# Visit 9 instead of visit 8 for the second rows' reciprocal, product and turns, in an attention and feed-forward kernel on one Trainium2 core

## The chip, the cores and the metric

The kernel runs on one core of one Trainium2 chip. A core has TensorE (PE in the profile; PEld is its weight load), VectorE (DVE), ScalarE (ACT), GpSimd (POOL) and SyncE (SP), which here only issues DMAs. Results of PE land in a memory of eight banks, PSUM; DVE and ACT empty the banks. The metric is the device time of one execution in microseconds, as the median of several runs.

## The reference

Two attention steps on `x` (4 batches of 12480 tokens with 128 channels, 32 inducing rows), then a feed-forward layer with a leaky ReLU of 2048 units:

```python
def mab(q, kv):
    s = scale * (q @ kv.transpose(0, 2, 1))
    s = s - s.max(-1, keepdims=True)
    a = np.exp(s)
    a /= a.sum(-1, keepdims=True) + 1e-09
    return a @ kv
h = mab(I, x)               # I: the inducing rows, for each batch
y = mab(x, h)               # 4 x 12480 x 128
...
h = y @ w_in                # 49920 x 2048
g = np.maximum(h, 0.0) + alpha * np.minimum(h, 0.0)
return g @ w_out
```

## The kernel before, in words

**Rows, blocks, visits.** The tokens of a batch are cut into groups of 16 tiles of 128 tokens; the code calls one such group `(b, s)`: batch `b`, rows `s`. "First rows" is `(0, 0)`, "second rows" `(0, 1)`. A group has four blocks of four tiles (512 tokens). Each block is visited four times; a visit computes four chunks of 128 of the 2048 hidden units for the block's 512 tokens. Visits are numbered through: 0 to 15 are the first rows, 16 to 31 the second rows, and so on. The part ahead of visit 0 (loads, the first attention step of batch 0) is a list of steps written out by hand.

**One visit.** `visit` takes four banks (`hh`) and issues four matmuls side by side, each with 32 rows of the attention weights `a2` and of the product `HW` (inducing output times `w_in`), L808. Then the four banks are emptied with a ReLU into bf16 tiles `gt`, on ACT (L821) or DVE (L823). In the same turn of the loop `second` multiplies the `gt` of the visit before by the output weights, 16 matmuls (L834), into the block's accumulator bank `bp`. `linear` adds the linear part of the leaky ReLU for a pair of blocks (L861): at visit 8 for blocks 0 and 1, at visit 12 for blocks 2 and 3. So PE's order is: the four L808 of visit n, now and then L861, the sixteen L834 of visit n-1, then what the tasks of visit n add.

**Finishing a block.** `finish` reads the accumulator bank into an output tile `ob` and issues its DMA from SP (L894). For the first four blocks the attention weights are not yet normalised, so there `ob` is the accumulator times the reciprocal `rec` of the sums (DVE, L880); later blocks are plain copies. `rec` is made at visit 7 (DVE, L1173) from a tree of sums on POOL. `blocks[0].later` holds block 0 back: it is finished at visit 8, just before block 1, which `second` finishes in the same turn of the loop.

**Preparing the next rows.** While a group is visited, the attention weights of the next are made by eight tasks, each put at a visit: `b_scores` (16 small matmuls, L644, and a copy to SBUF), `b_max` (DVE, L721), `b_less_pool` (POOL, L726), `b_exp` (ACT, L688), `b_sum` (five additions on POOL, L712, and L736, which gives `den`), `b_rec` (the reciprocal `rc` of `den`, DVE, L749), `b_mul` (POOL, L758, makes `rep`, the weights repeated four times in bf16) and `b_turn` (a transposing DMA from SP, L766, into `a2`, whose tile is `a<-rep` in the profile). For the second rows product and turn come in two halves of eight tiles. The list `when` in the planning loop says at which visit each of the eight stands. Visit 16 is the first to read the second rows' `a2`, and only its first half; visit 24 is the first to read the other half.

**What decides the order.** Each engine runs its instructions in the order in which the program issues them; nothing is reordered at run time. A planner (`Plan.choose`) runs at build time: with a beam search over estimated costs it decides for each visit which of the four ReLUs go to ACT and which to DVE, on which engine a copy runs, whether a task's DVE or ACT work stands at the end of its visit ("n") or in the middle of the next visit's ReLUs ("l", run by `run_waiting` ahead of the third ReLU), and which of the eight banks each tile takes. Moving a task therefore may also change those choices nearby. A task's own semaphore waits are placed by the framework: an instruction that waits holds up what is behind it on its engine, and SP's DMAs are issued strictly one after the other.

Of the kernel before, what the change touches and what calls it, by code (L numbers as in the profile page):

```python
# [30 lines left out]
def kernel(  # L31
# [654 lines left out]
    def b_exp(e, n):  # L686
        def work():
            nc.scalar.activation(out=e[:, :n], in_=e[:, :n], func=EXP, scale=scale)  # L688

        plan.then(work)  # L690
# [512 lines left out]
    def at(n, fn, *args, cost=()):  # L1203


        todo.setdefault(max(n, 0), []).append((fn, args, cost))
# [12 lines left out]
    for b, s, nt in groups[1:]:  # L1219
        n = first[b, s]  # L1220
        when = [n - 23, n - 19, n - 16, n - 14, n - 13, n - 11, n - 9, n - 6]
        if (b, s) == (0, 1):
            when = [0, 2, 3, 6, 7, 8, 8, 8]
        if (b, s) == (0, 2):
            when[7] = n - 7
        at(when[0], on, b, b_scores, s, nt, cost=[("s", 25 * nt), ("f", 0)])
        at(when[1], on, b, b_max, s, nt, cost=[("v", 70 + 33 * nt)])
        at(when[2], on, b, b_less_pool, s, nt)
        at(
            when[3],  # L1230
            lambda b=b, s=s, nt=nt: b_exp(states[b].e2[s], nt),
            cost=[("a", 100 + 27 * nt)],
        )
        at(when[4], on, b, b_sum, s, nt)
        at(when[5], on, b, b_rec, s, nt, cost=[("v", 160)])
        parts = [(0, H), (H, H)] if (b, s) in ((0, 1), (0, 2)) else [(0, nt)]
        for t0, n in parts:
            at(when[6], on, b, b_mul, s, n, t0)
            if when[6] == when[7]:
                at(when[7], on, b, b_turn, s, t0, n)  # L1240
        if when[6] != when[7]:
            for t0, n in parts:
                at(when[7], on, b, b_turn, s, t0, n)
# [130 lines left out]
```

## Time and profile before

| | |
|---|---|
| median of 3 runs | 593.95 us (593.32, 593.95, 594.05) |
| the profiled execution's own time | 593.45 us |
| its span in the trace | 591.7 us |
| around the span | 1.75 us |
| granted TensorE clock | 0.999 of full speed |
| PE busy | 584.9 us (99%) |
| DVE, ACT busy | 534.6 us (90%), 537.8 us (91%) |
| POOL busy | 216.9 us (37%) |
| visit 0 starts at | 30.04 us of the span |

In the trace, times are counted from the start of the span. A row of the timeline has the start, the duration, the engine, the source line, the operation, the tiles written and read with their shapes, and how many equal instructions were merged into the row; in square brackets stands how long the engine was idle before it and who ended that. A q after an engine's name stands for its queue, where DMAs are issued. The chain of waits is followed back from the last instruction of the program: at each step to what released it, or to the instruction before it on its engine. A busy PE is not PE at its peak, since the ends of matmuls are modelled; the starts of successive rows tell the pace.

### The profile page before, as it was taken

The numbers are of one execution on the slowest core, as the hardware profiler recorded it, in microseconds if no ns is written. First come the engines' busy times: TensorE is split into PE (matmuls) and PEld (weight loads), VectorE is DVE, ScalarE is ACT, GpSimd is POOL, SyncE is SP. The second block draws the span as 40 slices with busy tenths as digits, with TensorE's granted clock in tenths as the row PEclk, the third lists the DMA queues.
The fourth block names the chain that finished last, engine by engine and source line by source line (L and its number), as shares of the span: only waits on it lengthen the run. The fifth ranks groups of instructions, "written<-read, shape, count | busy, mean of one in ns | idle before, by whom it ended". The sixth has DMA issues, their size and how long they took to land.

```text
span 591.7 us, 23147 instructions
## 1 busy us (share of the span) xinstructions
PE 584.9 (99%) x9500; PEld 441.2 (75%) x9500; DVE 534.6 (90%) x977; ACT 537.8 (91%) x1086; POOL 216.9 (37%) x262
## 2 busy tenths in 40 slices
PE   8999999999999999999999999999999999999997
PEld 6677777777777777777777777777777777777776
DVE  5889999998999899999999899999999899999996
ACT  5788999999999999998999999999998998999985
POOL 3484543523325426413226256124034134144110
PEclk9999999999999999999999999999999999999999
DMA  8957699533188999532257999741331331432421
GB/s 335 278 184 171 149 244 202 134 89 88 38 236 159 212 194 219 118 82 67 80 151 186 183 238 224 139 100 38 91 77 51 92 77 52 119 83 58 91 69 47
DMA packets 122411, 80.56 MB, mean 136 GB/s; under 512 B 103824, under 2 KB 106176, under 8 KB 119232
## 3 DMA queue, kind: packets, MB, share of 16 engines
q1 hardware_dynamic: 122080, 78.99, 55.0%
q8 instruction: 74, 1.21, 0.9%
q14 instruction: 33, 0.27, 0.2%
q10 hardware_dynamic: 224, 0.09, 0.1%
HBM read 28.07 MB, written 25.56 MB: 91 GB/s over the span
## 4 chain that ended last, share of the span: by engine, by line
PE 91%; DVE 1%; DVEq 0%; issue 0%; ACT 0%
PE bp L834 64%; PE hh L808 21%; PE bp L861 2%; PE hh L644 1%; PE hh L473 1%; PE hh L379 1%; DVE gt L823 0%; DVE ob L880 0%; DVEq L1369 0%; PE hh L598 0%; PE hh L521 0%; DVE s L393 0%; PE hh L582 0%; PE hh L567 0%; PE hh L518 0%
## 5 line engine op out<-in xcount | busy, mean ns | idle before, releaser
L821 ACT ACTIVATE gt<-hh 128x512 bf16<-128x512 f32 x852 | 454.4, 605 | 35.2 <-PE hh L808 29.6
L823 DVE TENSOR_SCALAR gt<-hh 128x512 bf16<-128x512 f32 x708 | 454.3, 684 | 25.1 <-PE hh L808 14.3
L834 PE MATMUL bp<-W,gt 128*128 128x128 bf16 x6240 | 417.1, 220 | 0.2 <-DVE gt L823 0.2
L834 PEld LDWEIGHTS <-gt 128*128 128x128 bf16 x6240 | 349.3, 98 | 84.9 <-issue 77.0
L808 PE MATMUL hh<-a,HW 32*128 32x512 bf16 (+2 forms) x1664 | 156.4, 370 | 0.3 <-DVE ob L880 0.2
L758 POOL TENSOR_TENSOR rep<-e,rc 128x2048 bf16<-128x2048 f32 (+2 forms) x26 | 84.8, 3263 | 24.6 <-DVE rc L749 24.2
L726 POOL TENSOR_TENSOR e<-e,smx 128x512 f32<-128x512 f32 (+1 forms) x24 | 24.6, 1025 | 155.8 <-ACT gt L821 73.2
L808 PEld LDWEIGHTS <-HW 32*128 32x128 bf16 x1664 | 40.4, 91 | 42.0 <-issue 6.2
L712 POOL TENSOR_TENSOR t<-e 128x256 f32<-128x256 f32 (+1 forms) x24 | 17.2, 717 | 140.1 <-ACT e L688 140.1
L887 ACT COPY ob<-bp 128x512 f32<-128x512 f32 x64 | 37.5, 585 | 4.6 <-PE bp L834 1.4
L712 POOL TENSOR_TENSOR t<-t 128x128 f32<-128x128 f32 (+3 forms) x100 | 30.3, 303 | 7.8
L330 POOL CAST xn<-xs 128x2048 bf16<-128x2048 f32 x17 | 32.1, 1888 | 2.1 <-DMA xs<-in_x_dram 1.6
L889 DVE COPY ob<-bp 128x512 f32<-128x512 f32 x30 | 20.6, 686 | 5.2 <-PE bp L834 5.2
L393 DVE TENSOR_SCALAR_CACHE_REDUCE s<-hh 128x512 f32<-128x512 f32 (+2 forms) x29 | 18.0, 619 | 1.6 <-PE hh L379 1.6
L861 PEld LDWEIGHTS <-a 32*128 32x128 bf16 x392 | 15.0, 93 | 5.7
L861 PE MATMUL bp<-HA,a 32*128 32x128 bf16 x392 | 19.1, 214 | 0.0
L418 ACT ACTIVATE e1T<-s,rm 128x512 bf16<-128x512 f32 (+1 forms) x25 | 18.0, 719 | 0.7 <-DVE rm L402 0.7
L721 DVE TENSOR_REDUCE smx<-e 128x16 f32<-128x512 f32 (+1 forms) x24 | 15.9, 662 | 0.0
L963 PE MATMUL bp<-blank 128*128 128x256 bf16 x78 | 14.2, 318 | 1.2 <-DVE blank L909 1.2
L688 ACT ACTIVATE e<-e 128x512 f32<-128x512 f32 (+1 forms) x24 | 15.0, 626 | 0.0
L489 DVE SCALAR_TENSOR_TENSOR hs<-hs,fac,hh 128x128 f32<-128x128 f32 (+1 forms) x25 | 8.6, 344 | 6.4 <-PE hh L473 5.8
L702 ACT COPY e<-hh 128x512 f32<-128x512 f32 (+1 forms) x22 | 13.4, 607 | 0.0
(109 smaller groups left out, 204.5 us busy)
## 6 DMA issues: line engine op xcount, KB each, us to landing
out_dram<-ob SPq DMA_DIRECT2D x97, 256.0 KB, 2.5
xs<-in_x_dram SPq DMA_DIRECT2D x23, 1024.0 KB, 6.4
xs<-in_x_dram SPq DMA_DIRECT2D x2, 512.0 KB, 9.0
w_in_f<-in_moe_w_in_dram SPq DMA_DIRECT2D x1, 1024.0 KB, 4.8
a<-rep SPq DMA_TRANSPOSE x27, 4.8
xT<-xn SPq DMA_TRANSPOSE x18, 6.4
e<-e1T SPq DMA_TRANSPOSE x18, 3.8
xs_left<-in_x_dram SPq DMA_DIRECT2D x4, 64.0 KB, 5.2
```

Source lines behind the costliest of these rows:

```text
L330: nc.gpsimd.tensor_copy(out=st.xn[s][:], in_=xs[:])
L393: nc.vector.tensor_scalar(out=s1[:parts, :cols], in0=ps[:parts, :cols], scalar1=-scale, scalar2=None, op0=MULT, op1=MIN, accum_out=st.mx[: ...
L712: nc.gpsimd.tensor_tensor(out=t[:, :n], in0=src[:, :n, :w], in1=src[:, :n, w : 2 * w], op=ADD)
L726: nc.gpsimd.tensor_tensor(out=st.e2[s][:, :n], in0=st.e2[s][:, :n], in1=st.m2[s][:, :n].unsqueeze(2).broadcast_to([P, n, M]), op=SUB,)
L758: nc.gpsimd.tensor_tensor(out=st.rep[s][:, ts], in0=st.e2[s][:, ts].unsqueeze(2).broadcast_to([P, n, R, M]), in1=rc[:, ts].unsqueeze(2).un ...
L808: nc.tensor.matmul(hh[:, q * cols + w.start : q * cols + w.stop], HWs[b][rows, v * P : (v + 1) * P], a2[rows, t0 : t0 + nt, :].rearrange(" ...
L821: nc.scalar.activation(out=gt[:, :cols], in_=hh[:, :cols], func=RELU)
L823: nc.vector.tensor_relu(gt[:, :cols], hh[:, :cols])
L834: nc.tensor.matmul(blk.acc[:, t * C : (t + 1) * C], gt[:, (q * nt + t) * P : (q * nt + t + 1) * P], W1[:, k, :], start=(not blk.begun), st ...
L861: nc.tensor.matmul(blk.acc[w, t * C : (t + 1) * C], blk.a2[rows, blk.t0 + t, w], HAs[b][rows, :], start=(not blk.begun and t == 0), stop=F ...
L887: nc.scalar.copy(out=ob[:, :nt], in_=acc)
L889: nc.vector.tensor_copy(out=ob[:, :nt], in_=acc)
```

## The change

The last three tasks of the second rows, `b_rec`, `b_mul` and `b_turn`, are put at visit 9 and not at visit 8. Their order among themselves stays, the halves are kept, and nothing else in the source differs.

```diff
         if (b, s) == (0, 1):
-            when = [0, 2, 3, 6, 7, 8, 8, 8]
+            when = [0, 2, 3, 6, 7, 9, 9, 9]
```

With that the built program has its instructions in another order near visits 7 to 10. The number of instructions is the same on every engine. Each row below is one engine's order, from the ReLUs of visit 7 to those of visit 10; the number in brackets is the visit of a ReLU.

```
DVE before: relu(7) relu(7) rec relu(8) relu(8) rc ob0 ob1 relu(9) relu(10) relu(10)
DVE after:  relu(7) relu(7) rec relu(8) ob0 ob1 relu(9) rc relu(10) relu(10)
ACT before: relu(7) exp relu(7) relu(8) relu(8) relu(9) x3 copy(scores) relu(10) x2
ACT after:  relu(7) relu(7) exp relu(8) x3 relu(9) x3 copy(scores) relu(10) x2
SP before:  turn xT, turn a first half, turn a second half, out block 0, out block 1, turn xT left, turn xT
SP after:   turn xT, out block 0, out block 1, turn a first half, turn a second half, turn xT left, turn xT
```

Here `exp` is the second rows' `b_exp`, `rc` their reciprocal, `ob0` and `ob1` the scaled outputs of blocks 0 and 1. The planner now puts `ob0` and `ob1` at the end of visit 8's own ReLUs, where before they stood in the middle of visit 9's. It also gives the first two ReLUs of visit 7 to ACT (before: the second and third) and the first three of visit 8 (before: the first two). Visit 9 and all visits from 10 on keep their division between ACT and DVE. The four `hh` banks of visit 10 were before, in order: one emptied by DVE in visit 8, that of block 0's accumulator, one emptied by ACT in visit 9, and that of block 1's accumulator. After the change they are one emptied by ACT in visit 8, one emptied by ACT in visit 9 (its first ReLU), that of block 1's accumulator, and another emptied by ACT in visit 9 (its second ReLU). From visit 12 on, all but eight tiles of some 1700 follow the same tile in their bank as before. POOL's order does not change at all.

## The prediction

> **What bounds the kernel now.** The page comes first: which engine fills the span, and what the chain of waits is made of.
>
> ```profile
> span 591.7 us, 23147 instructions
> PE 584.9 (99%) x9500; PEld 441.2 (75%) x9500; DVE 534.6 (90%) x977; ACT 537.8 (91%) x1086; POOL 216.9 (37%) x262
> PE 91%; DVE 1%; DVEq 0%; issue 0%; ACT 0%
> ```
>
> PE is the bound: 91% of the chain is its own. A change on DVE, POOL or SP is worth only what it takes from PE's waiting. So the second view is PE's own waits over the whole span (who was waited for; total, times, longest, in us).
>
> ```profile
> PE bp L963 <- DVE blank L909: 1.2, 1, 1.2
> PE hh L364 <- POOL w_in_f L1036: 0.7, 1, 0.7
> PE hh L808 <- DVE ob L880: 0.2, 1, 0.2
> PE bp L834 <- DVE gt L823: 0.2, 1, 0.2
> PE hh L967 <- ACT ind_b L956: 0.2, 1, 0.2
> ```
>
> L963, L967 and L364 belong to the hand-written part ahead of visit 0. In the visits there are two waits: one for a `gt` (L834) and one of L808 on `ob` (L880), which the diff touches. Its 0.2 us counts only the time without any running matmul, so I measure the hole by the pace of the visits, in the timeline around it.
>
> ```profile
> 41.92 0.39 PE L861 MATMUL bp<-HA,a 32*128 32x128 bf16 x8
> 42.23 1.07 PE L834 MATMUL bp<-W,gt 128*128 128x128 bf16 x16
> 43.23 0.40 PE L808 MATMUL hh<-a,HW 32*128 32x512 bf16 x4
> 43.56 1.07 PE L834 MATMUL bp<-W,gt 128*128 128x128 bf16 x16
> 44.95 0.86 PE L808 MATMUL hh<-a,HW 32*128 32x512 bf16 x3
> 46.02 0.37 PE L808 MATMUL hh<-a,HW 32*128 32x512 bf16 x1 [0.21 <-DVE ob L880]
> 46.32 1.07 PE L834 MATMUL bp<-W,gt 128*128 128x128 bf16 x16
> 47.32 0.40 PE L808 MATMUL hh<-a,HW 32*128 32x512 bf16 x4
> 48.65 0.40 PE L808 MATMUL hh<-a,HW 32*128 32x512 bf16 x4
> 54.17 0.40 PE L808 MATMUL hh<-a,HW 32*128 32x512 bf16 x4
> ```
>
> Visit 8 ends with the L834 at 42.23; visits 9, 10, 11, 12 start at 43.23, 44.95, 47.32, 48.65, and visit 16 at 54.17. Visit 11 takes 48.65 - 47.32 = 1.33 us, an undisturbed visit without extra work. Visit 10 has no extra work either, and takes 47.32 - 44.95 = 2.37 us. **The hole is 2.37 - 1.33 = 1.04 us.** Its four L808, issued together elsewhere (0.40 for all four), come out in pieces, the last at 46.02, because their banks come free late. What holds them is on the other engines:
>
> ```profile
> 42.03 0.24 DVE L1173 RECIPROCAL rec<-den 128x16 f32<-128x16 f32 x1
> 42.18 1.28 DVE L823 TENSOR_SCALAR gt<-hh 128x512 bf16<-128x512 f32 x2
> 44.57 0.25 DVE L749 RECIPROCAL rc<-den 128x16 f32<-128x16 f32 x1 [1.10 <-POOL den L736]
> 44.74 1.22 DVE L880 TENSOR_TENSOR ob<-bp,rec 128x512 f32<-128x512 f32 x2
> 45.88 3.99 DVE L823 TENSOR_SCALAR gt<-hh 128x512 bf16<-128x512 f32 x6
> 40.78 0.60 ACT L821 ACTIVATE gt<-hh 128x512 bf16<-128x512 f32 x1
> 41.28 0.62 ACT L688 ACTIVATE e<-e 128x512 f32<-128x512 f32 x1
> 41.80 1.56 ACT L821 ACTIVATE gt<-hh 128x512 bf16<-128x512 f32 x3
> 43.72 1.57 ACT L821 ACTIVATE gt<-hh 128x512 bf16<-128x512 f32 x3 [0.35 <-PE hh L808]
> 41.98 0.73 POOL L712 TENSOR_TENSOR t<-e 128x256 f32<-128x256 f32 x1 [1.06 <-ACT e L688]
> 42.78 1.46 POOL L712 TENSOR_TENSOR t<-t 128x128 f32<-128x128 f32 x4
> 44.96 3.75 POOL L758 TENSOR_TENSOR rep<-e,rc 128x1024 bf16<-128x1024 f32 x2 [0.43 <-issue]
> ```
>
> Read it backwards. L808 waits for `ob`, whose two products are done at 44.74 + 1.22 = 45.96. They could have run much earlier: `rec` is there at 42.27, block 0's accumulator is complete with the L861 at 42.31, block 1's with the L834 at 43.30. But on DVE they stand behind `rc`, and `rc` waits 1.10 us, until 44.57, for POOL's `den`, the end of a tree that started at 41.98, when ACT's `exp` had ended (41.28 + 0.62).
>
> **The change part by part.** No instruction is added or removed, so the sum has only moved waits. I follow the new order with the durations above, and a start-to-start step of 0.48 for ACT's ReLUs ((1.56 - 0.60)/2) and 0.60 for DVE's (1.28 less a ReLU's 0.68).
>
> *DVE.* After `rec` comes one ReLU of visit 8 (42.18), then `ob0` at 42.8, done 43.4, and `ob1`, which needs 43.30 and starts about 43.4, done 44.1. Then visit 9's ReLU, done 44.7. Both accumulator banks are free 1.9 us earlier than 45.96. The wait on `den` has not gone: it now stands in front of visit 10's ReLUs.
>
> *ACT and POOL.* Two ReLUs of visit 7 now precede `exp`, so `exp` is one step late: 41.76, and with it the tree, `den`, `rc` (45.05 to 45.30), the product (45.44) and the turns, all +0.48. Visit 8's three ReLUs run 42.28 to 43.84 (the third of them was on DVE). Its `gt` is used by the ninth L834 after 43.56, at 44.06 with 1.00/16 each: in time. Visit 9's ReLUs start at 43.72 as before; the 0.35 us that ACT idled there took up the extra one.
>
> *Visit 10 on PE, 44.95.* Its four banks: visit 8's third ReLU (43.84), `ob1` (44.1), visit 9's first (44.32) and second (44.80) on ACT. From a bank's last read to PE's start is 0.06 (45.96 to 46.02), so 44.86: **no wait, 0.09 us to spare.**
>
> *Visit 10's ReLUs.* Results arrive 0.49 after PE's start (43.23 to 43.72): 45.44. `rc` is done at 45.30, so its wait costs DVE nothing: 0.14 us to spare. The first ReLU ends at 46.12; visit 11 (44.95 + 1.33 = 46.28) needs that bank: 46.18, 0.10 to spare. The cover of `rc` is thus thin: if `den` came later by d, PE would lose about d - 0.24.
>
> *SP and DMA.* SP's queue, in order:
>
> ```profile
> 40.87 3.68 SPq L356 DMA_TRANSPOSE xT<-xn  x1
> 46.88 3.09 SPq L766 DMA_TRANSPOSE a<-rep  x2
> 50.06 1.01 SPq L894 DMA_DIRECT2D out_dram<-ob  x2
> ```
>
> The outputs were ready at 45.96 and left at 50.06 behind the turns. Now SP is free at 44.55 and issues them at once (1.01 for both), done by 45.6, ahead of the turns, which wait for the product until 46.88 + 0.48 = 47.36. So the outputs cost the turns no issue time. Landing of the turns here, of all turns and of all outputs, in that order:
>
> ```profile
> DMA to landing us min/median/max: 3.0/3.0/3.1
> ...
> DMA to landing us min/median/max: 2.7/4.8/6.6
> ...
> DMA to landing us min/median/max: 2.0/2.5/7.8
> ```
>
> The first half, 47.36 + 3.1 = 50.5, is needed by visit 16 at 54.17 - 1.04 = 53.13: 2.6 us of cover; the second half by visit 24. Even the longest landing, 6.6, would cost 53.96 - 53.13 = 0.83, less than the gain. Nothing here reaches PE.
>
> *POOL beside a busy DVE.* Before, DVE idled while the tree ended; now it runs `ob` there. The price lies between nothing and the tree waiting out both products, 1.22. A later tree shows which:
>
> ```profile
> 61.13 1.46 POOL L712 TENSOR_TENSOR t<-t 128x128 f32<-128x128 f32 x4
> 61.19 3.22 DVE L823 TENSOR_SCALAR gt<-hh 128x512 bf16<-128x512 f32 x5
> ```
>
> The four smaller additions take 1.46 there beside five ReLUs, and 1.46 at 42.78, half of it beside an idle DVE. I take nothing, the nearer row, and keep 1.22 for the range.
>
> **Sum:** PE -1.04 (visit 10), +0 on the other steps. PE's waits after visit 10 come to one of 0.2, so nothing later takes the gain back. Profiled execution: 593.45 - 1.04 = 592.41. That execution lies 0.50 under the median (593.95) and the three runs spread over 0.73, so the median comes out between 592.41 and 592.91. I forecast **592.7**.
>
> **The rivals.**
>
> *Part of the hole stays.* The three covers in a row are 0.09, 0.14 and 0.10 us. If visit 9's ReLUs on ACT start one step later (0.48) behind visit 8's third, visit 10 waits 0.48 - 0.09 = 0.39: gain 0.65, **593.1** from the forecast. For it: ACT carries one ReLU more before 43.7. Against: its idle 0.35 there, and that visit 8's results come early enough.
>
> *The wait only moves.* `rc` still stands on DVE, now ahead of two ReLUs that PE needs. If the tree waits out both products beside it (1.22), PE loses 1.22 - 0.24 = 0.98, and the gain is 0.06: **593.7**. Then the change doesn't do what its order promises. Against it: the tree's 1.46 at 61.13.
>
> *Slower: the outputs hold back the turns.* They now go ahead of the turns while the turn issued at 40.87 is still moving. The second leaves SP at about 45.2. With the longest landing of any output, 7.8, it is done at 53.0; if the first turn can only then move (3.1), it lands at 56.1, and visit 16 waits 56.1 - 53.13 = 2.9: net +1.9, 593.45 + 1.9 = **595.3**. It costs from a landing after 50.0 on, and the kernel is slower than before from 51.1 on, 5.9 us after the issue. Against: the median output lands in 2.5, and the turn has its own time on the queue, 2.2 us after the second output. The Trainium skill, "DMA: Bandwidth & Descriptors", section on queues, rings and completion order, says that each DMA engine takes descriptors in ring order, while completions need not come in that order; by this rule a turn does stand behind an output's remaining bytes. In this trace no turn closely follows an output that lands late, so it does not bear the rule out or refute it.
>
> **How the numbers follow.** The hole closes wholly: 0.72. Part stays: 0.13. The wait only moves: 0.09. Slower: 0.06. Range 592.0 to 594.0: its low end is 592.41 less about half the spread of the runs, its high end is no gain, at the median; it leaves out the slower rival and the tails. About 0.2%, here 1.19 us, is what a measurement can tell from no change. The forecast gain lies at this bound: 1.04 by the trace, 593.95 - 592.7 = 1.25 by the medians. So the first case splits by the scatter of the runs, 0.45 over the bound and 0.27 under it; the second and third fall within 0.2%. Faster 0.45, same 0.49, slower 0.06.
>
> **What would show it.** Visit 10 to visit 11 takes 1.33, with four L808 in one row; no PE wait for `ob`; `ob` on DVE at about 42.8 and 43.4; `rc` near 45.05 with a short idle time before it; the first turn near 47.4, landing before 51; the outputs at 44.6. Wrong would be an L808 of visits 10 or 11 waiting for an ACT or DVE `gt`, `rc` starting after 45.3, or a wait at visit 16 for a DMA.

## The result and the profile after

| | before | after |
|---|---|---|
| median of 17 runs | 593.43 us (593.05 to 594.05) | 592.37 us (592.06 to 592.92) |
| ratio after to before | | 0.9982, 95% interval 0.9975 to 0.9990 |
| the profiled execution | 593.45 us | 592.39 us |
| its span | 591.7 us | 590.6 us |

The kernel is 1.06 us faster, just under the 0.2% that the prediction set as its bound (1.19 us); the interval does not reach 1. That outcome lay on the line the prediction had drawn (0.45 for over the bound, 0.49 for under it), and its range reached up to no gain; so it is the visits below, and not the time, that bear out the mechanism. In the two profiled executions the difference is 593.45 - 592.39 = 1.06 as well. PE's waits over the whole span, in the profile after (who was waited for; total, times, longest):

```profile
PE bp L963 <- DVE blank L909: 1.2, 1, 1.2
PE hh L364 <- POOL w_in_f L1036: 0.7, 1, 0.7
PE bp L834 <- DVE gt L823: 0.2, 1, 0.2
```

The row of L808 on `ob` is gone, and no row has come in its place. (The row of L967, from the part ahead of visit 0, is gone too; visit 0 starts at 30.03, before at 30.04.) The timeline after, at the visits that the prediction went through:

```profile
41.68 0.39 PE L808 MATMUL hh<-a,HW 32*128 32x512 bf16 x4
43.22 0.39 PE L808 MATMUL hh<-a,HW 32*128 32x512 bf16 x4
44.94 0.40 PE L808 MATMUL hh<-a,HW 32*128 32x512 bf16 x4
46.27 0.40 PE L808 MATMUL hh<-a,HW 32*128 32x512 bf16 x4
47.60 0.40 PE L808 MATMUL hh<-a,HW 32*128 32x512 bf16 x4
...
53.12 0.40 PE L808 MATMUL hh<-a,HW 32*128 32x512 bf16 x4
```

Visits 8, 9, 10, 11 and 12 start there, and visit 16 at 53.12. Visit 10 issues its four L808 in one piece and takes 46.27 - 44.94 = 1.33 us, where before it took 2.37. All of the 1.04 us is visit 10's. Visit 16 comes 54.17 - 53.12 = 1.05 earlier, and the last L834 of the span 1.03 earlier, so nothing gives it back: six visits between 98 and 334 differ by 0.06 to 0.31 us, in both directions, and add up to 0.02. The other engines at that place, from the same timeline:

```profile
42.01 0.24 DVE L1173 RECIPROCAL rec<-den 128x16 f32<-128x16 f32 x1
42.21 0.69 DVE L823 TENSOR_SCALAR gt<-hh 128x512 bf16<-128x512 f32 x1
42.81 1.28 DVE L880 TENSOR_TENSOR ob<-bp,rec 128x512 f32<-128x512 f32 x2
44.01 0.68 DVE L823 TENSOR_SCALAR gt<-hh 128x512 bf16<-128x512 f32 x1
45.08 0.25 DVE L749 RECIPROCAL rc<-den 128x16 f32<-128x16 f32 x1 [0.39 <-POOL den L736]
45.44 3.38 DVE L823 TENSOR_SCALAR gt<-hh 128x512 bf16<-128x512 f32 x5
...
41.77 0.63 ACT L688 ACTIVATE e<-e 128x512 f32<-128x512 f32 x1
42.28 3.04 ACT L821 ACTIVATE gt<-hh 128x512 bf16<-128x512 f32 x6
...
42.48 0.73 POOL L712 TENSOR_TENSOR t<-e 128x256 f32<-128x256 f32 x1 [1.69 <-ACT e L688]
45.47 3.75 POOL L758 TENSOR_TENSOR rep<-e,rc 128x1024 bf16<-128x1024 f32 x2 [0.43 <-PE hh L808]
...
44.44 1.82 SPq L894 DMA_DIRECT2D out_dram<-ob  x2
47.39 3.08 SPq L766 DMA_TRANSPOSE a<-rep  x2
```

DVE still waits for POOL's `den`, 0.39 us instead of 1.10, but both outputs are now ahead of that wait: they end at 42.81 + 1.28 = 44.09, before visit 10 asks for a bank at 44.94. The wait sits where it delays nothing: `rc` ends at 45.33, and the next ReLU starts at 45.44. On ACT the six ReLUs of visits 8 and 9 now follow each other without the idle time.

### The profile page after: what moved, and what is told of

It reads as the page before. It is cut to its first block, busy times and chain, and to the rows that moved or that the text cites. A ratio compares the mean times of both kernels' runs of the same rounds, so it can differ in the third digit from the quotient of the medians.

```text
span 590.6 us, 23148 instructions
## 1 busy us (share of the span) xinstructions
PE 584.2 (99%) x9500; PEld 441.2 (75%) x9500; DVE 534.7 (91%) x976; ACT 537.8 (91%) x1087; POOL 216.7 (37%) x262
## 4 chain that ended last, share of the span: by engine, by line
PE 95%; DMA 3%; DVE 1%; ACT 0%; DVEq 0%; issue 0%; POOL 0%; SPq 0%
PE bp L834 66%; PE hh L808 22%; DMA xs<-in_x_dram 3%; PE bp L861 2%; PE hh L644 2%; PE hh L473 1%; PE hh L379 1%; PE bp L963 0%; PE hh L598 0%; DVE gt L823 0%; DVEq L1369 0%; PE hh L364 0%; DVE xT L372 0%; DVE xn L349 0%; PE hh L582 0%; PE hh L521 0%
## 5 line engine op out<-in xcount | busy, mean ns | idle before, releaser
L834 PE MATMUL bp<-W,gt 128*128 128x128 bf16 x6240 | 417.2, 220 | 0.2 <-DVE gt L823 0.2
L834 PEld LDWEIGHTS <-gt 128*128 128x128 bf16 x6240 | 349.3, 98 | 84.4 <-issue 76.4
L808 PE MATMUL hh<-a,HW 32*128 32x512 bf16 (+2 forms) x1664 | 155.6, 370 | 0.0
L808 PEld LDWEIGHTS <-HW 32*128 32x128 bf16 x1664 | 40.3, 91 | 41.6 <-issue 5.8
```

The costliest lines, as they stand in the source:

```text
L808: nc.tensor.matmul(hh[:, q * cols + w.start : q * cols + w.stop], HWs[b][rows, v * P : (v + 1) * P], a2[rows, t0 : t0 + nt, :].rearrange(" ...
L834: nc.tensor.matmul(blk.acc[:, t * C : (t + 1) * C], gt[:, (q * nt + t) * P : (q * nt + t + 1) * P], W1[:, k, :], start=(not blk.begun), st ...
```

## The experiments

The theory under test: the hole of 1.04 us was made by `rc` waiting for `den` on DVE with both outputs queued behind it. The rivals: that the gain comes from SP's order (outputs ahead of the turns), or from the planner's new choices near visits 7 to 9. Each kernel below was timed in five rounds beside the kernel before; its ratio is to that one.

### Only the product and the turns moved

```diff
-            when = [0, 2, 3, 6, 7, 8, 8, 8]
+            when = [0, 2, 3, 6, 7, 8, 9, 9]
```

> Only the product and the turns go to visit 9; the reciprocal rc stays at visit 8, ahead of both outputs on DVE. Theory (rc's wait on den, with the outputs behind it, makes the hole): visit 10 keeps its 1.04 us hole, rc idles about 1.1 us again, ratio to before 1.000. Rival (the outputs' DMAs going ahead of the turns on SP, or the later product, bring the gain): the time of the change, ratio 0.998, no PE wait for ob.

Measured: 593.73 us against 593.42, ratio 1.0003 (0.9994 to 1.0012). Its timeline, DVE, PE around visits 10 and 11, and SP:

```profile
44.31 0.25 DVE L749 RECIPROCAL rc<-den 128x16 f32<-128x16 f32 x1 [1.10 <-POOL den L736]
44.48 1.22 DVE L880 TENSOR_TENSOR ob<-bp,rec 128x512 f32<-128x512 f32 x2
...
44.69 0.86 PE L808 MATMUL hh<-a,HW 32*128 32x512 bf16 x3
45.76 0.37 PE L808 MATMUL hh<-a,HW 32*128 32x512 bf16 x1 [0.20 <-DVE ob L880]
47.06 0.40 PE L808 MATMUL hh<-a,HW 32*128 32x512 bf16 x4
...
45.60 1.82 SPq L894 DMA_DIRECT2D out_dram<-ob  x2
47.51 2.66 SPq L766 DMA_TRANSPOSE a<-rep  x2
```

The hole is back whole: 47.06 - 44.69 - 1.33 = 1.04. Yet in this kernel SP does issue the outputs ahead of the turns, at 45.60 and 46.22 against 47.51. So SP's order alone is worth nothing here, and the place of `rc` is what the gain hangs on.

### The change, with the outputs behind the turns

```diff
-                nc.sync.dma_start(out=ov[:, t0 : t0 + nt, :], in_=ob[:, :nt])
+                def send():
+                    nc.sync.dma_start(out=ov[:, t0 : t0 + nt, :], in_=ob[:, :nt])
+
+                if blk.k < 2:
+                    sends.append(send)
+                else:
+                    send()
...
+    sends = []
+    at(9, lambda: [send() for send in sends])
```

> The change as it is, but the output DMAs of blocks 0 and 1 are issued behind the second rows' turns, as before the change. Theory: the place of these DMAs is worth nothing, since PE does not wait for them: ratio 0.998, visit 10 takes 1.33 us, the outputs leave SP near 50.5. Rival (part of the gain is the outputs leaving 5 us earlier): ratio nearer to 1.000, or an ob waiting for its buffer.

Measured: 592.53 us against 593.42, ratio 0.9986 (0.9977 to 0.9995). The outputs left SP at 50.71 and 51.33, 6 us later than in the change (L895 is L894 moved by a line), and visit 10 takes 46.40 - 45.07 = 1.33:

```profile
45.07 0.39 PE L808 MATMUL hh<-a,HW 32*128 32x512 bf16 x4
46.40 0.39 PE L808 MATMUL hh<-a,HW 32*128 32x512 bf16 x4
...
47.53 3.09 SPq L766 DMA_TRANSPOSE a<-rep  x2
50.71 1.01 SPq L895 DMA_DIRECT2D out_dram<-ob  x2
```

This is the other half of the same test: the old SP order keeps the gain. The ratio is 0.0004 above the change's, inside both intervals.

### The change, with the planner's choices of before

```diff
-            self.taken = iter("".join(reversed(taken)))
+            taken.reverse()
+            taken[9] = taken[9][:R] + taken[8][R + 2] + taken[9][R:]
+            taken[8] = taken[8][: R + 2] + taken[8][R + 3 :]
+            self.taken = iter("".join(taken))
...
+        if n == 8:
+            chains.insert(0, [("v", 160)])
+        if n == 9:
+            assert chains.pop(0) == [("v", 160)]
```

> The change with the planner's choices of before (which engine takes which ReLU, the outputs in the middle of visit 9, the same banks): only rc, product and turns move. Theory: the outputs run from 43.4 to 44.65 on DVE, free before 44.95, so the hole closes without the planner's reshuffle: ratio 0.998, visit 10 takes 1.33 us, and exp runs at 41.28 as before. Rival (the outputs' earlier place, which the planner chose, is what closes the hole): a hole of 0.3 us or more.

The second part of the edit makes the planner reckon with `rc` at visit 8, as before; the first then moves `rc` alone to visit 9.

Measured: 592.53 us, ratio 0.9977 (0.9966 to 0.9989). From its timeline (L883, L752 and L811 are L880, L749 and L808 moved by three lines):

```profile
43.65 1.28 DVE L883 TENSOR_TENSOR ob<-bp,rec 128x512 f32<-128x512 f32 x2
45.44 0.24 DVE L752 RECIPROCAL rc<-den 128x16 f32<-128x16 f32 x1
...
45.21 0.39 PE L811 MATMUL hh<-a,HW 32*128 32x512 bf16 x4
46.54 0.39 PE L811 MATMUL hh<-a,HW 32*128 32x512 bf16 x4
```

With the same engines, the same banks and the outputs still in the middle of visit 9, the hole closes all the same: the outputs end at 44.93, 0.28 us before visit 10. The planner's reshuffle was not needed. `rc` has no idle time at all here: `exp` keeps its old place, so `den` comes earlier than in the change, and DVE comes to `rc` later, after two ReLUs of visit 8 and not one.

### The kernel before, with exp one visit earlier

```diff
-            when = [0, 2, 3, 6, 7, 8, 8, 8]
+            when = [0, 2, 3, 5, 7, 8, 8, 8]
```

> The kernel before, with the second rows' exp one visit earlier (5, not 6), so that den comes earlier; rc stays at visit 8 ahead of the outputs. Theory: POOL's tree can start at 40.92, when the first rows' sums are done, and takes 2.55, so rc runs near 43.5 with hardly a wait, the outputs end near 44.95, and visit 10's hole shrinks from 1.04 to about 0 to 0.1: ratio 0.998. Rival (the place in the order and not the wait on den makes the hole): a hole of 0.5 or more, ratio 0.999 to 1.000.

Measured: 592.08 us, ratio 0.9978 (0.9969 to 0.9987). `rc` stays at visit 8, ahead of the outputs:

```profile
43.41 0.25 DVE L749 RECIPROCAL rc<-den 128x16 f32<-128x16 f32 x1 [0.40 <-POOL den L736]
43.58 1.22 DVE L880 TENSOR_TENSOR ob<-bp,rec 128x512 f32<-128x512 f32 x2
...
40.13 0.73 PE L808 MATMUL hh<-a,HW 32*128 32x512 bf16 x4
...
45.05 0.39 PE L808 MATMUL hh<-a,HW 32*128 32x512 bf16 x4
46.38 0.39 PE L808 MATMUL hh<-a,HW 32*128 32x512 bf16 x4
```

The order that made the hole is kept, only `den` comes earlier, and visit 10 takes 1.33. So it is the length of the wait, not the order by itself. The planner gave one more ReLU of visit 8 to ACT here too, as in the change; the kernel with the planner's choices held shows that this is not needed to close the hole. The price is at visit 7 (40.13): its four L808 take 0.73, in the change 0.43. That ACT, held up by the earlier `exp`, empties the banks later is the likely reason; it was not tried. From visit 20 to the last L834 this kernel is also 0.5 us shorter than the change; visit 306 alone takes 1.33 there against 1.64. The planner may have chosen other banks for it; that was not tried. By the two intervals this kernel can't be told from the change.

### Longer waits for den

```diff
+        if (st.b, s) == (0, 1):
+            for _ in range(1):                  # second kernel: 2
+                t = e2_pool.tile([P, ST, M // 2], f32, name="t16", tag="t16")
+                nc.gpsimd.tensor_tensor(
+                    out=t[:], in0=st.e2[s][:, :, : M // 2], in1=st.e2[s][:, :, M // 2 :], op=ADD
+                )
         src = b_tree(st.e2[s], n)
```

> The change with the first addition of the second rows' tree done once more on POOL (its result is the same), so den comes one step later, 0.8 us. Theory: the covers behind rc are 0.11 (rc to visit 10's first ReLU) and 0.09 (that ReLU's bank to visit 11), so PE loses 0.8 - 0.2 = 0.6 us: about 593.0, with L808 or L834 of visit 11 waiting for a DVE gt. Rival (DVE has room enough behind rc): no loss, 592.4.

> The change with the first addition of the second rows' tree done twice more on POOL (its result is the same), so den comes 1.6 us later. Theory: PE loses 1.6 - 0.2 = 1.4 us, more than the change gained: about 593.8, ratio 1.000 to 1.001. Rival (no cover is used up, or DVE catches up): less than 0.5 us, 592.9 or below.

Measured: 592.85 us, ratio 0.9990 (0.9980 to 1.0001), with one addition more, and 593.58 us, ratio 1.0000 (0.9991 to 1.0010), with two. The kernel with one (L755 is `rc`, L814 the visits 10, 11 and 12):

```profile
46.05 0.25 DVE L755 RECIPROCAL rc<-den 128x16 f32<-128x16 f32 x1 [1.10 <-POOL den L742]
...
45.21 0.40 PE L814 MATMUL hh<-a,HW 32*128 32x512 bf16 x4
46.53 0.74 PE L814 MATMUL hh<-a,HW 32*128 32x512 bf16 x4
48.27 0.40 PE L814 MATMUL hh<-a,HW 32*128 32x512 bf16 x4
```

And the kernel with two:

```profile
46.98 0.25 DVE L755 RECIPROCAL rc<-den 128x16 f32<-128x16 f32 x1 [1.77 <-POOL den L742]
...
46.79 0.39 PE L814 MATMUL hh<-a,HW 32*128 32x512 bf16 x3
47.83 0.37 PE L814 MATMUL hh<-a,HW 32*128 32x512 bf16 x1 [0.65 <-DVE gt L829]
49.20 0.40 PE L814 MATMUL hh<-a,HW 32*128 32x512 bf16 x4
```

`rc`'s idle time grew by 1.10 - 0.39 = 0.71 and 1.77 - 0.39 = 1.38; visit 11 grew from 1.33 to 48.27 - 46.53 = 1.74 and 49.20 - 46.79 = 2.41, that is by 0.41 and 1.08. Both differences are 0.30: so much of a later `den` is covered, and what is beyond it was lost one for one in both kernels. The expectations had losses of 0.6 and 1.4: an addition held `den` up by 0.7 us and not by 0.8, and the cover is 0.30 and not 0.20. The place is as expected, visit 11's fourth bank, held by the ReLU behind `rc`. The second kernel has lost the whole gain: the idle row on DVE is again long, only the victim is another.

### The turns later still

```diff
-            when = [0, 2, 3, 6, 7, 9, 9, 9]
+            when = [0, 2, 3, 6, 7, 10, 11, 11]  # second kernel: 12, 12, 12
```

> The change with rc at visit 10 and product and turns at visit 11. Theory: rc no longer waits for den at all; the product starts near 47.1, the first turn is issued near 49.0 and lands 3.0 to 4.6 us later, at 52.0 to 53.6, against visit 16 at 53.1: no loss, or up to 0.5 us; ratio 0.998 to 0.999. Rival (a later turn must cost by its whole delay): 1.6 us more than the change, ratio above 1.000.

> The change with rc, product and turns at visit 12. Theory: rc near 48.8, the first turn issued near 51.0, landing at 54.0 to 55.6, so visit 16 waits 0.9 to 2.5 us for it: 593.3 to 594.9, about as slow as before the change or slower; the wait shows as L808 on the turn's DMA. Rival (the cover ahead of visit 16 is longer than read from the landing): no wait, ratio 0.998.

Measured: 593.11 us, ratio 0.9997 (0.9984 to 1.0010), for 10 and 11; 595.18 us, ratio 1.0023 (1.0010 to 1.0036), for 12. SP's turns and visits 15 and 16, of the first:

```profile
50.99 3.08 SPq L766 DMA_TRANSPOSE a<-rep  x2
...
53.43 0.39 PE L808 MATMUL hh<-a,HW 32*128 32x512 bf16 x4
55.84 0.40 PE L808 MATMUL hh<-a,HW 32*128 32x512 bf16 x4 [1.01 <-DMA a<-rep]
```

And of the second:

```profile
51.24 3.08 SPq L766 DMA_TRANSPOSE a<-rep  x2
...
52.00 0.40 PE L808 MATMUL hh<-a,HW 32*128 32x512 bf16 x4
55.70 0.40 PE L808 MATMUL hh<-a,HW 32*128 32x512 bf16 x4 [2.31 <-DMA a<-rep]
```

Here PE waits for the turn, as the prediction's slower rival would have it, though for another reason than the outputs. With 12 the wait is 55.70 - 52.00 - 1.33 = 2.37, within the 0.9 to 2.5 expected; the median is 0.3 above the expected times, the ratio (times 593.36, 594.7) is not. That median hides two groups: eight of the twelve executions show a granted clock of 0.995 to 0.997 and take 595.1 to 596.2, the other four, at 0.998 to 1.000, take 593.4 to 594.4, the profiled one (594.38) among them. In the kernel before, timed beside it, 5 of 35 have so low a clock; whether the wait brings it on was not tried. With 10 and 11 the expectation failed: the wait is 55.84 - 53.43 - 1.33 = 1.08, and I had allowed 0.5. The first turn was issued at 50.99 in an execution whose visits all come 1.64 us later than in the change, so at 49.35 by the change's clock, 0.3 later than I had it, and it landed 4.80 us after its issue, not 3.0 to 4.6. (The 1.64 arose ahead of visit 0, and this profiled execution, 594.54, is 1.4 above the median.) The last section looks at the landing. Both kernels are also 0.57 us shorter than the change in the visits behind visit 20, 306 above all, as the one with `exp` earlier is; so their times show less than the waits: 2.37 - 0.57 = 1.80 with 12, 0.5 with 10 and 11.

## Why the prediction was right, point by point

- *The hole.* 1.04 us by the pace of the visits, and 1.04 is what visit 10 lost. PE's own wait row said 0.2; the pace was the right measure.
- *DVE.* `ob` was forecast at 42.8 and 43.4, and stands at 42.81, ending at 44.09; `rc` at 45.05, and stands at 45.08 behind 0.39 us of idle time. That `rc` was the cause, and neither SP nor the planner, was argued in the prediction and is shown by the first three experiments; the fourth shows that the length of its wait is what counted.
- *ACT and POOL.* `exp` was forecast at 41.76 (41.77), the product at 45.44 (45.47). The first rival, a part of the hole left by a late ACT, fell narrowly: visit 9's ReLUs started at 43.72 as forecast, and the second ended at 44.84 (forecast 44.80), 0.10 us before visit 10. With the 0.06 from a bank's last read to PE's start, 0.04 was to spare. POOL's tree was not slowed by the outputs beside it: from its start to `rc` passed 45.08 - 42.48 = 2.60, before 44.57 - 41.98 = 2.59. So the second rival fell as it was priced; the experiments with longer waits show that its place was right, and that its cover is 0.30 where the prediction had 0.24.
- *SP and DMA.* The outputs left at 44.44 (forecast 44.55) and held SP for 1.82 us, not 1.01, which the turn, free only at 47.39, didn't notice. The first turn landed at 50.42, 2.7 us ahead of visit 16, the second at 53.83. The slower rival needed an output landing 5.9 us after its issue; they took 3.59 and 3.56, longer than the median of 2.5. Where the outputs left nearer to the turn, the second of them 1.3 and 1.6 us ahead of it in the kernels of the first and third experiment and not 2.3, it landed after 3.59 and 3.78 us and not 3.03. So the rival's mechanism may show there, at a small price; that it is the outputs was not tried.
- *The sum.* 593.45 - 1.04 = 592.41 against 592.39 for the profiled execution. The term that was mis-sized is the step from there to the median: I put the median 0.3 above the profiled execution, since the median of the three runs shown lay 0.50 above it. Over 17 runs the median before is 593.43, within 0.02 of the profiled execution, and the forecast of 592.7 is 0.33 too high. By the trace alone the gain was 1.04 of 593.45, or 0.175%, under the bound.

## What to carry to other kernels

An instruction that waits costs what stands behind it on its engine, so look there for work that is ready and that another engine needs, and move the waiting instruction behind it. The wait itself need not become shorter: here it was cut from 1.10 to 0.39, and a wait of 1.10 in the new place cost 0.41 where it had cost 1.04 in the old. Then measure what cover is left behind the new place, because it is used up one for one, and how far back the result is needed: two visits further on, the turn itself came too late.

## What the runs showed of the hardware

The landing of the same half turn (eight tiles, the same bytes) varies more than I had used. In the kernel before, the change, and the kernels with a longer `den` the first of the two landed 3.03 to 3.04 us after its issue; with the turns at visits 11 and 12 it took 4.80 and 4.42, and with the planner held 3.78, and 5.71 for the second. What the DMA engines moved between issue and landing tells these apart. Of the first turn in the kernel before (46.88 to 49.92; a row has the queue, its packets, MB, and share of the 16 engines' time):

```profile
q1 hardware_dynamic: 1060, 0.26, 44.9%
```

and of the first turn in the kernel with the turns at visit 11 (50.99 to 55.79; packets of the turns issued behind it are counted too):

```profile
q1 hardware_dynamic: 1914, 0.48, 71.3%
q8 instruction: 1, 0.02, 1.3%
q14 instruction: 1, 0.01, 0.7%
```

The packet on the queue that the profile names q8 instruction has 16 KB; it started at 53.76 and took 1.00 us. In the kernel before, the 32 packets of 4 bytes that close the turn go off 2.37 to 2.57 us after its issue. Here 30 of them go off after 2.36 to 2.58 us, and the last two only after 3.75.

The ten traces have twenty such turns of the second rows. Eight landed after 3.03 or 3.04 us, and none of these had an instruction packet between issue and landing. Ten had one, and took 3.38 to 5.71; all seven beyond 4 us are among them. The other two (3.59 and 3.78) had the outputs close ahead of them. In all ten kernels the packet comes within 0.4 us of the start of visit 15, and every turn that was still in flight then landed late, so a cover read from one landing can be up to 2.7 us too long (5.71 against 3.04). This is read from the traces alone: no kernel moved the instruction packet and nothing else.
